# Reciprocals as exp(-ln), dealt feature steps, a weight chunk on another queue and a last product in halves: one change to a gated mix of two attention blocks

## Chip, core and metric

The kernel runs on one core of a Trainium2 chip. The metric is device time in microseconds (us): the median of repeated executions of the whole program. Beside these times there is one profiled execution, whose trace gives the start and length of each instruction on each engine.

The engines are named as the profile names them: PE is TensorE (PEld its weight loads), DVE is VectorE, ACT is ScalarE, POOL is GpSimd, SP is SyncE, which here only issues DMAs. A "q" after a name is the engine's own queue or sequencer.

## What is computed

Two attention blocks read the same x (2048 rows, 1024 columns, 32 heads of 32). A is a linear attention with the feature map phi, B a local one that looks at 8 earlier positions, 2 apart. A sigmoid gate mixes them. (The weights and x are bf16. `z` is the einsum as it stands, a sum over the sequence.)

```python
def A(x, wqkv, wo):
    q, k, v = split_heads(x @ wqkv)
    phi = lambda t: jnp.where(t > 0, t + 1, jnp.exp(t)) + 1e-6
    pq, pk = phi(q), phi(k)
    kv = jnp.einsum("bhsd,bhse->bhde", pk, v)
    z = jnp.einsum("bhsd->bhd", pk)
    num = jnp.einsum("bhqd,bhde->bhqe", pq, kv)
    den = jnp.einsum("bhqd,bhd->bhq", pq, z)[..., None] + 1e-6
    return heads_to_rows(num / den) @ wo

def B(x, wqkv, wo):
    q, k, v = split_heads(x @ wqkv)
    # logits over 8 gathered keys, 2 apart, masked below 0
    attn = softmax(logits * Dh ** -0.5)
    return heads_to_rows(attn @ gathered_v) @ wo

g = sigmoid((x * gate_w).sum(-1, keepdims=True))
out = g * A(x, A_wqkv, A_wo) + (1 - g) * B(x, B_wqkv, B_wo)
```

## The kernel before

**Products.** x is transposed by DMA into xT (`xt_load`, L89 to L92). Even and odd rows of x are kept apart (`xpar`), since B looks back in steps of 2. Most of the large products are done in a seven-product scheme of 2x2 blocks (class `Group`, L236): products m1 to m7 of sums and differences of blocks of x and of the weights, accumulated in PSUM tiles X and Y, with intermediate saves M1s, U2s and U4s by ScalarE (`save`, L256) and evacuations by VectorE that add a save to a PSUM tile (`acc`, L228). The sums of x and of the weights are VectorE operations at L102 to L105 and L133 to L136. `run` (L393) interleaves the products of one group with m3 and m4 of the group before. PSUM holds four banks for these products (X0, X1, Y0, Y1), and one slot of four banks (`side_ps`, L323) that everything else shares: B's scores `s`, B's attention output `o`, A's key-value product `kps`, A's output `oA`.

**Order.** The order on TensorE and on SP is that of the program text. The instructions of the other engines are put in order by a scheduler that respects dependencies. After each product `side` (L350) moves the program's own clock on by one step and does two things. It deals one VectorE operation from lists that were handed to `defer` (L361), placed behind the last evacuation (`dve_side`, L371). And it may advance one of the side generators: B's attention (`attn`, L641), A's key-value product (`kv`, L526), A's output (`out` in `qa_out`, L564).

**Stages by the profile's clock.** Up to 24 us: B's value projection of the first pairs in plain form (`vb_plain`, L464), while DMAs bring x and the first weights, and warm-up matmuls (`warm_up`, L431) fill the wait. To 66 us: the rest of B's values and the first keys and queries. To about 303 us: B's keys and queries by columns, alternating with A's keys and values by rows, and B's attention in between. To about 356 us: A's queries in plain form (`qa_plain`, L605) with A's output. To 387 us: the last queries together with the first output products. To the end: the output products of eight pairs (`out_group`, L783). The last pair's group has `last` set, which puts m5 ahead of m7; its last product is m4.

**First loads.** SP issues, in this order, the transpose of x tile 0, the four chunks of the first half of B's value weights (`vb_load(k, 0)`, 256 KB each), the transposes of tiles 4, 1 and 5, the four chunks of the second half, and further transposes (L184 to L193). ScalarE's first instruction is a table load (L79).

**A's key features.** When one row tile of A's keys is complete, `done` in `ka_group` calls `phi` (L498): an Exp on ScalarE (L500) and three VectorE operations, the maximum with 0 (L504), the minimum with 1 plus eps (L505), and the sum (L506). They are issued at once, all three together. There are 16 such tiles. The `kv` generator of the same pair, one or more groups later, reads the result.

**A's output.** For each 128 columns of queries and each half (16 times), `out` multiplies the query features `eq` with KVz (L575), ScalarE copies the PSUM result to `of` or `ofv` (L577), GpSimd adds eps to the 33rd column of each head (L580) and multiplies by `nel` (L581), VectorE takes the reciprocal (L583), and GpSimd multiplies the numerators by it in two operations (L586). A store to DRAM follows (L588). `nel` holds exp(-gate), so that dividing by it gives the gate's ratio g/(1-g); the factor 1-g (`omg`) is applied at the very end. The query features are made of an Exp by ScalarE (L622) and VectorE operations (L625, L627), which release the PSUM bank.

**The end.** Each output tile is evacuated by `final` of `out_group` (L806 to L814), by ScalarE or VectorE into `osb` (128x512), and stored by SP.

Of the kernel before, what the change touches and what calls it, by code (L numbers as in the profile page):

```python
# [8 lines left out]
ACT = mybir.ActivationFunctionType  # L9
ALU = mybir.AluOpType  # L10
# [3 lines left out]
F32 = mybir.dt.float32  # L14
P = 128
# [3 lines left out]
SPAN = 3 * TW  # L19
EPS = 1e-6  # L20
RATE_R = 0.8
RELU_ACT = (False, False)
OA_DELAY = 5
RATE_Q = 1.0
RATE_O = 1.3
# [3 lines left out]
def kernel(  # L29
# [11 lines left out]
    nc = tc.nc  # L41
# [11 lines left out]
    outpar = out[0].rearrange("(j p) d -> p j d", p=2)  # L53

    def xrows(t):
        return xpar[t // 8, (t % 8) * P:(t % 8 + 1) * P, :]

    consts = ctx.enter_context(tc.tile_pool(name="consts", bufs=1))
# [10 lines left out]
    ps_pj = ctx.enter_context(tc.tile_pool(name="ps_pj", bufs=1, space=bass.MemoryType.PSUM))  # L69
# [19 lines left out]
    def xt_load(t):  # L89
        p, j = divmod(t, 8)  # L90
        hf, c = divmod(j, 4)
        nc.sync.dma_start_transpose(out=xT[p][:, :, hf, c * P:(c + 1) * P], in_=xrows(t))  # L92
# [81 lines left out]
    W = wp.tile([P, 8, D], BF16, name="W", tag="W")  # L174
# [4 lines left out]
    nc.gpsimd.dma_start(out=gw[:], in_=gate_w.rearrange("(k p) -> p k", p=P))  # L179

    def vb_load(k, j):
        nc.sync.dma_start(out=W[:, 2 * k:2 * k + 2, 512 * j:512 * j + 512],
                          in_=bview[:, 2 * k:2 * k + 2, 2 * D + 512 * j:2 * D + 512 * j + 512])
    xt_load(0)  # L184
    for k in range(4):
        vb_load(k, 0)
    for t in (4, 1, 5):
        xt_load(t)
# [30 lines left out]
    nc.gpsimd.memset(bd[:], 0.0)  # L219
    for i in range(4):  # L220
        nc.gpsimd.memset(bd[32 * i:32 * i + 32, i, :], 1.0)
    nel = consts.tile([P, 16], F32, name="nel")
    omg = consts.tile([P, 16], F32, name="omg")
    KVz = consts.tile([P, 8, 132], BF16, name="KVz")

    last_dve = [None]

    def acc(out_, ps, add):  # L228
        if add is None:
            nc.scalar.copy(out=out_, in_=ps)  # L230
        else:
            last_dve[0] = nc.vector.tensor_tensor(out=out_, in0=ps, in1=add, op=ALU.add).ins  # L232
# [3 lines left out]
    class Group:  # L236
# [37 lines left out]
        def m6(self):  # L274
            self.mm(self.X, 6, False)
            self.U2s = self.save(self.X, "U2s", self.scale[1])

        def m7(self):
            self.Y = self.ps("Y")
            self.mm(self.Y, 7, True)  # L280
            if self.last:
                self.final(1, 1, self.Y[:], self.U4s[:])

        def m5(self):
            self.mm(self.X, 5, False)
# [8 lines left out]
                self.row_done(0)  # L294

        def m4(self):
            self.mm(self.Y, 4, False)
            self.final(1, 0, self.Y[:], self.U2s[:])
            if self.row_done:
                self.row_done(1)  # L300

    def row_ops(w, pair):
        p, c = divmod(pair, 4)
        return lambda m, kc: (xop(m, kc, p, slice(c * P, c * P + P)), w.get(m, kc))
# [18 lines left out]
    def side_ps(name):  # L323
        return ps_s.tile([P, 4, 512], F32, name=name, tag="s")
# [36 lines left out]
    def defer(products, ops, gap=1):  # L361


        deferred.append([state["now"] + products, list(ops), gap])
# [46 lines left out]
    def tile_of(pair, i):  # L411
        return (pair // 4) * 8 + (pair % 4) + 4 * i
# [3 lines left out]
    gps = gps_tile[:, 0, 0:16]  # L416
# [6 lines left out]
                             start=kc == 0, stop=kc == 7)  # L423

    def gate_end():
        nc.scalar.activation(out=nel[:], in_=gps, func=ACT.Exp, scale=-1.0)
        nc.scalar.activation(out=omg[:], in_=gps, func=ACT.Exp)
        nc.vector.tensor_scalar(out=omg[:], in0=omg[:], scalar1=1.0, scalar2=None, op0=ALU.add)
        nc.vector.reciprocal(out=omg[:], in_=omg[:])
# [65 lines left out]
                    vb_store(vs[pair], pair, i)  # L495


    def phi(e, t, relu_on_act=False):  # L498

        nc.scalar.activation(out=e, in_=t, func=ACT.Exp)  # L500
        if relu_on_act:
            nc.scalar.activation(out=t, in_=t, func=ACT.Relu)
        else:
            nc.vector.tensor_scalar(out=t, in0=t, scalar1=0.0, scalar2=None, op0=ALU.max)  # L504
        nc.vector.tensor_scalar(out=e, in0=e, scalar1=1.0, scalar2=EPS, op0=ALU.min, op1=ALU.add)  # L505
        nc.vector.tensor_tensor(out=e, in0=e, in1=t, op=ALU.add)  # L506

    pks = {}
    kv_state = {"n": 0}
# [1 line left out]
    def ka_group(w, pair):  # L511
        ts = [tring.tile([P, D], BF16, name="tA", tag="t") for _ in range(2)]

        def final(i, j, ps, add):
            acc(ts[i][:, 512 * j:512 * j + 512], ps, add)

        def done(i):
            e = ering.tile([P, D], BF16, name="eA", tag="e")
            phi(e[:], ts[i][:])
            pks[tile_of(pair, i)] = e  # L520
        return Group(row_ops(w, pair), final, done)

# [34 lines left out]
    def cols_of(ap, nn, n=1):  # L557

        return ap.rearrange("(n r) (c e) -> r n c e", n=n, c=4)[:, :, nn, :]
# [3 lines left out]
    def qa_out(es, nn, p):  # L563
        def out(i):  # L564
            yield 0, 2
            oa["n"] += 1
            if oa["n"] % 3 and not any(e[4] == "attn" for e in queue):
                of = vwp.tile([P, 4, 8, 33], F32, name="ofv", tag="vw")
            else:
                of = ofp.tile([P, 4, 8, 33], F32, name="of", tag="of", bufs=1)  # L570
            rec = smallp.tile([P, 4, 8, 1], F32, name="rec", tag="rec")
            o = side_ps("oA")
            for k in range(4):
                for j in range(2):
                    nc.tensor.matmul(o[:, k, 132 * j:132 * j + 132], lhsT=es[i][:, j, k * P:(k + 1) * P],  # L575
                                     rhs=KVz[:, nn + 4 * j, :], start=True, stop=True)
            oa["copy"] = nc.scalar.copy(out=of[:].rearrange("p n h e -> p n (h e)"), in_=o[:, :, 0:264]).ins  # L577
            yield 1, 2
            t = 8 * p + 4 * i
            nc.gpsimd.tensor_scalar(out=rec[:, :, :, 0], in0=of[:, :, :, 32], scalar1=EPS, scalar2=None, op0=ALU.add)  # L580
            nc.gpsimd.tensor_tensor(out=rec[:, :, :, 0], in0=rec[:, :, :, 0],  # L581
                                    in1=nel[:, t:t + 4, None].broadcast_to([P, 4, 8]), op=ALU.mult)
            nc.vector.reciprocal(out=rec[:], in_=rec[:])  # L583
            ob = tring.tile([P, 4, 8, 32], BF16, name="obA", tag="t")
            for k in range(0, 4, 2):
                nc.gpsimd.tensor_tensor(out=ob[:, k:k + 2], in0=of[:, k:k + 2, :, 0:32],  # L586
                                        in1=rec[:, k:k + 2].broadcast_to([P, 2, 8, 32]), op=ALU.mult)
            nc.sync.dma_start(out=cols_of(OA_d[p][i][:, :], nn, 4),  # L588
                              in_=ob[:].rearrange("p k h e -> p k (h e)"))
        return out  # L590

    def qa_group(w, nn, p):
        ts = [tring.tile([P, 2, 512], BF16, name="tq", tag="t") for _ in range(2)]
        es = [ering.tile([P, 2, 512], BF16, name="eq", tag="e") for _ in range(2)]
        out = qa_out(es, nn, p)

        def final(i, j, ps, add):
            acc(ts[i][:, j, :], ps, add)

        def done(i):  # L600
            phi(es[i][:], ts[i][:], RELU_ACT[i])
            add_side(OA_DELAY, out(i), p, "oa")
        return Group(col_ops(w, p), final, done)

# [178 lines left out]
    def out_group(pair, parts):  # L783
        p, c = divmod(pair, 4)

        def operands(m, kc):
            assert m in (1, 2, 4) or ("o", id(parts)) in ready, (pair, m)
            n, c4 = divmod(kc, 4)
            o, S, o16, n0 = parts[min(n, len(parts) - 1)]
            n -= n0  # L790
            if m == 1:
                l = o[:, 0, n, 2 * c4]
            elif m == 2:
                l = o[:, 0, n, 2 * c4 + 1]
            elif m == 4:
                l = o[:, 1, n, 2 * c4 + 1]
            elif m == 7:
                l = o16[:, 1, n, 2 * c4]
            else:
                l = S[:, {5: 0, 6: 1, 3: 2}[m], n, c4]  # L800
            return l, Wo["AB"[n + n0]].get(m, c4)

        ts = [tile_of(pair, i) for i in range(2)]
        sc = [omg[:, t:t + 1] for t in ts]

        def final(i, j, ps, add):  # L806
            osb = ering.tile([P, 512], BF16, name="osb", tag="e")
            if add is None:
                nc.scalar.activation(out=osb[:], in_=ps, func=ACT.Copy, scale=sc[i])
            else:  # L810
                last_dve[0] = nc.vector.scalar_tensor_tensor(out=osb[:], in0=ps, scalar=sc[i], in1=add,  # L811
                                                             op0=ALU.mult, op1=ALU.add).ins
            r0 = (ts[i] % 8) * P
            nc.sync.dma_start(out=outpar[p, r0:r0 + P, 512 * j:512 * j + 512], in_=osb[:])  # L814
        return Group(operands, final, nk=8, scale=sc)


# [67 lines left out]
    cols = []  # L885
# [75 lines left out]
```

## Time and profile before

| | |
|---|---|
| median of 8 runs | 468.33 us (467.1 to 469.31) |
| profiled execution | 467.51 us |
| its span, first to last instruction | 465.6 us |
| granted TensorE clock | 1.0 throughout |
| 66 to 303 us: TensorE / VectorE / ScalarE busy | 229.7 / 160.4 / 154.2 us of 237 |
| 303 to 356 us: TensorE / VectorE / ScalarE / GpSimd | 50.1 / 39.7 / 25.8 / 34.9 us of 53 |
| 387 to 462 us: TensorE / VectorE / ScalarE | 74.7 / 25.7 / 17.2 us of 75 |

The 1.9 us between the profiled execution's time and its span lie outside the first and last instruction. Busy times of different engines overlap; an engine that is idle costs nothing unless another waits for it. Matmul ends are modelled in the profile: a 128x512 matmul is shown with 379 ns while eight in a row take 1.73 us, that is 0.216 us each.

How the lines below are read: a timeline line has start, duration (both us), engine, source line, operation, output tile, input tiles, shapes, and in brackets the idle time ahead of it with the instruction that ended it. A line of the waits table has who waited, for whom, and then us in total, number of times, and the longest.

### The profile page before, as it was taken

The page shows a single profiled execution, that of the slowest core. Times are in us where ns is not written, and L with a number is a line of the kernel's source. Part 1 is how long each engine was busy: PE and PEld are TensorE (multiplying, and loading weights), DVE is VectorE, ACT ScalarE, POOL GpSimd, SP SyncE. Part 2 cuts the span into 40 slices and gives each one's busy share as a digit, 9 for nine tenths or more (in the row PEclk, how much of TensorE's full clock was granted, in tenths as well). Part 3 has the DMA queues.
Part 4 walks back from the last instruction along what each step waited for, and adds up shares of the span by engine and source line. Part 5 has one row for each costly group of instructions (what it writes and reads, how often), then busy time and mean ns, then how long its engine had stood idle before and what let it go on. Part 6 is the DMA issues. An engine that isn't in the chain of part 4 may idle for free. (4 is left out here: it accounts for less than half of the span.)

```text
span 465.6 us, 11844 instructions
## 1 busy us (share of the span) xinstructions
PE 447.0 (96%) x5052; PEld 217.3 (47%) x5129; DVE 280.6 (60%) x458; ACT 230.2 (49%) x331; POOL 65.1 (14%) x145
## 2 busy tenths in 40 slices
PE   7989999999999999999999999999989999999997
PEld 5445444444444444444444444445545444444443
DVE  0546668769748587485774847578767763155211
ACT  1233447568468385683855848535554432222221
POOL 8000000000000000000000000008887521000000
PEclk9999999999999999999999999999999999999999
DMA  7999811590301703017020075373229971598111
GB/s 169 194 216 240 276 43 64 149 251 18 80 4 34 157 19 74 11 32 156 19 72 14 24 157 185 84 209 80 68 75 201 210 160 58 105 194 199 45 46 45
DMA packets 117653, 51.65 MB, mean 111 GB/s; under 512 B 77664, under 2 KB 115552, under 8 KB 117600
## 3 DMA queue, kind: packets, MB, share of 16 engines
q1 hardware_dynamic: 117504, 50.88, 46.8%
q8 instruction: 40, 0.66, 0.6%
q0 software_dynamic: 96, 0.01, 0.1%
q14 instruction: 13, 0.11, 0.1%
HBM read 25.69 MB, written 16.79 MB: 91 GB/s over the span
## 5 line engine op out<-in xcount | busy, mean ns | idle before, releaser
L617 PE MATMUL Q<-xT,WS 128*128 128x512 bf16 x246 | 57.7, 379 | 2.9 <-DVE eq L627 1.7
L250 PEld LDWEIGHTS <-xT 128*128 128x128 bf16 (+1 forms) x352 | 32.6, 98 | 38.3 <-issue 1.5
L250 PE MATMUL X<-T,SS 128*128 128x512 f16 x176 | 45.2, 379 | 0.0
L660 ACT ACTIVATE PT<-s 128x1368 bf16<-128x1368 f32 x24 | 31.5, 1311 | 20.1 <-PE s L654 20.0
L259 ACT COPY U4s<-X 128x512 f32<-128x512 f32 x38 | 22.1, 581 | 35.5 <-PE X L250 35.5
L250 PE MATMUL Y<-W,xT 128*128 128x512 bf16 (+1 forms) x143 | 37.4, 379 | 1.9 <-issue 1.1
L617 PEld LDWEIGHTS <-WS 128*128 128x128 bf16 x256 | 24.3, 98 | 29.4 <-issue 3.0
L250 PEld LDWEIGHTS <-WS 128*128 128x128 bf16 (+1 forms) x256 | 24.0, 98 | 29.2 <-issue 2.0
L250 PEld LDWEIGHTS <-SS 128*128 128x128 f16 x264 | 24.4, 98 | 27.8
L622 ACT ACTIVATE eq<-Q 128x512 bf16<-128x512 f32 x32 | 19.1, 598 | 32.0 <-PE Q L617 30.9
L662 DVE TENSOR_TENSOR PT<-PT,maskp 128x1368 bf16<-128x1368 bf16 x24 | 20.8, 868 | 20.8 <-ACT PT L660 20.8
L250 PE MATMUL Y<-xT,WS 128*128 128x512 bf16 (+1 forms) x128 | 32.9, 380 | 0.0
L250 PE MATMUL X<-SS,TS 128*128 128x512 f16 x128 | 32.8, 379 | 0.0
L250 PEld LDWEIGHTS <-oT 128*128 128x128 bf16 (+1 forms) x192 | 18.8, 98 | 22.8 <-issue 0.3
L250 PEld LDWEIGHTS <-TS 128*128 128x128 f16 x192 | 18.2, 98 | 22.1 <-issue 1.1
L259 ACT COPY M1s<-X 128x512 f32<-128x512 f32 x38 | 22.2, 584 | 11.8 <-PE X L250 9.1
L259 ACT COPY U2s<-X 128x512 f32<-128x512 f32 x38 | 22.1, 582 | 9.1 <-PE X L250 9.1
L685 DVE COPY nB<-o 128x684 f32<-128x684 f32 x24 | 20.8, 867 | 8.0 <-ACT rB L684 7.3
L586 POOL TENSOR_TENSOR obA<-ofv,rec 128x512 bf16<-128x512 f32 x22 | 23.7, 1099 | 8.2 <-DVE rec L583 7.6
L250 PE MATMUL Y<-W,oT 128*128 128x512 bf16 (+1 forms) x96 | 22.7, 379 | 0.0
L250 PE MATMUL X<-T,oS 128*128 128x512 f16 x96 | 22.7, 379 | 0.0
L250 PE MATMUL X<-W,SS 128*128 128x512 bf16 x79 | 22.2, 380 | 0.5
(125 smaller groups left out, 732.8 us busy)
## 6 DMA issues: line engine op xcount, KB each, us to landing
OB_d<-oB SPq DMA_DIRECT2D x24, 171.0 KB, 3.0
V_d<-va SPq DMA_DIRECT2D x16, 256.0 KB, 2.5
WS<-in_B_wqkv_dram SPq DMA_DIRECT2D x16, 256.0 KB, 4.3
W<-in_A_wqkv_dram SPq DMA_DIRECT2D x8, 512.0 KB, 6.1
OA_d<-obA SPq DMA_DIRECT2D x16, 256.0 KB, 2.3
out_dram<-osb SPq DMA_DIRECT2D x32, 128.0 KB, 1.8
oT<-OB_d SPq DMA_DIRECT2D x12, 256.0 KB, 4.8
vw<-V_d SPq DMA_DIRECT2D x8, 288.0 KB, 4.9
```

Of the source, the lines that this page charges most:

```text
L250: nc.tensor.matmul(ps[:], lhsT=lhsT, rhs=rhs, start=start and kc == 0, stop=kc == self.nk - 1, skip_group_check=True)
L259: nc.scalar.copy(out=s[:], in_=ps[:])
L586: nc.gpsimd.tensor_tensor(out=ob[:, k:k + 2], in0=of[:, k:k + 2, :, 0:32], in1=rec[:, k:k + 2].broadcast_to([P, 2, 8, 32]), op=ALU.mult)
L617: nc.tensor.matmul(ps[:], lhsT=w.W[:, kc, j * P:j * P + P], rhs=xT[p][:, kc, i, :], start=kc == 0, stop=kc == 7, skip_group_check=True)
L622: nc.scalar.activation(out=es[i][:, j, :], in_=ps[:], func=ACT.Exp)
L660: nc.scalar.activation(out=PT[:], in_=s[:, :, 0:TW], func=ACT.Exp, scale=SCALE)
L662: nc.vector.tensor_tensor(out=PT[:], in0=PT[:], in1=m[:, None, :].broadcast_to([P, 4, TW]), op=ALU.mult)
L685: nc.vector.tensor_copy(out=nB[:], in_=o[:, 0:4:2, 0:TW])
```

## The change

Five edits (names and lines are those of the kernel before, where it has them):

1. A's output. GpSimd's addition of eps and VectorE's reciprocal are gone. ScalarE now takes Ln of the denominator, with eps as its bias operand (a new 128x1 constant that GpSimd fills at the start), and then Exp of minus that, which is the reciprocal. GpSimd multiplies by `nel`, and `nel` is now exp(+gate), so that multiplying takes the place of dividing. The two multiplications by the numerators stay.
2. A's key features. `phi` issues its Exp and returns the three VectorE operations as a list. For A's keys the list goes to `defer(0, ...)`, so one is dealt per product, each behind the last evacuation. For the query features of `qa_group`, a function that the program does not use in its present plan, they are issued at once as before. The constant RELU_ACT, which was false for both, is gone.
3. The first chunk of the first weights is issued from ScalarE's queue, ahead of everything on SP; SP goes on with the transpose of x tile 0 and the other three chunks.
4. In the last group, m7 and m4 are each done in two halves of 256 columns. The halves lie in two PSUM banks (Y of this group and Y of the one before), and each half has its own evacuation and its own store.
5. `final` takes a range of columns for that.

```diff
     def vb_load(k, j):
-        nc.sync.dma_start(out=W[:, 2 * k:2 * k + 2, 512 * j:512 * j + 512],
+        (nc.scalar if (k, j) == (0, 0) else nc.sync).dma_start(out=W[:, 2 * k:2 * k + 2, 512 * j:512 * j + 512],
                           in_=bview[:, 2 * k:2 * k + 2, 2 * D + 512 * j:2 * D + 512 * j + 512])
+    vb_load(0, 0)
     xt_load(0)
-    for k in range(4):
+    for k in range(1, 4):
         vb_load(k, 0)
...
+    eps = consts.tile([P, 1], F32, name="eps")
+    nc.gpsimd.memset(eps[:], EPS)
...
+        def half(self, m, k, add, j):
+
+            h = slice(256 * k, 256 * k + 256)
+            if m == 7:
+                self.Ys.append(ps_pj.tile([P, 512], F32, name="Y", tag="Y" + str((self.par + k) % 2)))
+            for kc in range(self.nk):
+                lhsT, rhs = self.operands(m, kc)
+                nc.tensor.matmul(self.Ys[k][:, h], lhsT=lhsT, rhs=rhs[:, h], start=m == 7 and kc == 0,
+                                 stop=kc == self.nk - 1, skip_group_check=True)
+            self.final(1, j, self.Ys[k][:, h], add[:, h], h)
+
         def m7(self):
+            if self.last:
+                self.Ys = []
+                for k in range(2):
+                    self.half(7, k, self.U4s, 1)
+                return
             self.Y = self.ps("Y")
             self.mm(self.Y, 7, True)
-            if self.last:
-                self.final(1, 1, self.Y[:], self.U4s[:])
...
         def m4(self):
+            if self.last:
+                for k in range(2):
+                    self.half(4, k, self.U2s, 0)
+                return
...
     def gate_end():
-        nc.scalar.activation(out=nel[:], in_=gps, func=ACT.Exp, scale=-1.0)
+        nc.scalar.activation(out=nel[:], in_=gps, func=ACT.Exp)
...
-    def phi(e, t, relu_on_act=False):
+    def phi(e, t):
 
         nc.scalar.activation(out=e, in_=t, func=ACT.Exp)
-        if relu_on_act:
-            nc.scalar.activation(out=t, in_=t, func=ACT.Relu)
-        else:
-            nc.vector.tensor_scalar(out=t, in0=t, scalar1=0.0, scalar2=None, op0=ALU.max)
-        nc.vector.tensor_scalar(out=e, in0=e, scalar1=1.0, scalar2=EPS, op0=ALU.min, op1=ALU.add)
-        nc.vector.tensor_tensor(out=e, in0=e, in1=t, op=ALU.add)
+        return [lambda: nc.vector.tensor_scalar(out=t, in0=t, scalar1=0.0, scalar2=None, op0=ALU.max),
+                lambda: nc.vector.tensor_scalar(out=e, in0=e, scalar1=1.0, scalar2=EPS, op0=ALU.min, op1=ALU.add),
+                lambda: nc.vector.tensor_tensor(out=e, in0=e, in1=t, op=ALU.add)]
...
             e = ering.tile([P, D], BF16, name="eA", tag="e")
-            phi(e[:], ts[i][:])
+            defer(0, phi(e[:], ts[i][:]))
...
-            nc.gpsimd.tensor_scalar(out=rec[:, :, :, 0], in0=of[:, :, :, 32], scalar1=EPS, scalar2=None, op0=ALU.add)
+            nc.scalar.activation(out=rec[:, :, :, 0], in_=of[:, :, :, 32], func=ACT.Ln, bias=eps[:, 0:1])
+            nc.scalar.activation(out=rec[:, :, :, 0], in_=rec[:, :, :, 0], func=ACT.Exp, scale=-1.0)
             nc.gpsimd.tensor_tensor(out=rec[:, :, :, 0], in0=rec[:, :, :, 0],
                                     in1=nel[:, t:t + 4, None].broadcast_to([P, 4, 8]), op=ALU.mult)
-            nc.vector.reciprocal(out=rec[:], in_=rec[:])
...
-        def final(i, j, ps, add):
+        def final(i, j, ps, add, cols=slice(0, 512)):
...
-                last_dve[0] = nc.vector.scalar_tensor_tensor(out=osb[:], in0=ps, scalar=sc[i], in1=add,
+                last_dve[0] = nc.vector.scalar_tensor_tensor(out=osb[:, cols], in0=ps, scalar=sc[i], in1=add,
                                                              op0=ALU.mult, op1=ALU.add).ins
             r0 = (ts[i] % 8) * P
-            nc.sync.dma_start(out=outpar[p, r0:r0 + P, 512 * j:512 * j + 512], in_=osb[:])
+            nc.sync.dma_start(out=outpar[p, r0:r0 + P, 512 * j + cols.start:512 * j + cols.stop], in_=osb[:, cols])
```

More of the change, by code (lines that the diff above doesn't have):

```diff
@@ L21 @@
 RATE_R = 0.8
-RELU_ACT = (False, False)
 OA_DELAY = 5
@@ L600, in done @@
         def done(i):
-            phi(es[i][:], ts[i][:], RELU_ACT[i])
+            for f in phi(es[i][:], ts[i][:]):
+                f()
             add_side(OA_DELAY, out(i), p, "oa")
```

## The prediction, made before the changed kernel ran

> **What bounds the kernel now.** I read the busy shares first, then TensorE's waits, then the timeline around each wait.
>
> ```profile
> span 465.6 us, 11844 instructions
> ## 1 busy us (share of the span) xinstructions
> PE 447.0 (96%) x5052; PEld 217.3 (47%) x5129; DVE 280.6 (60%) x458; ACT 230.2 (49%) x331; POOL 65.1 (14%) x145
> ```
>
> TensorE is busy 96% of the span at full clock; nothing in the change removes a matmul. So the change can win only what lies in TensorE's 18.6 us of gaps (465.6 - 447.0) and at the two ends. The table of waits for TensorE alone (us in total, times, longest) says who ends those gaps:
>
> ```profile
> PE s L654 <- DVE nB L685: 2.0, 6, 0.7
> PE Q L617 <- DVE eq L627: 1.7, 1, 1.7
> PE gps L422 <- DMA xT<-in_A_x_dram: 1.6, 2, 1.0
> PE K L475 <- DMA W<-in_B_wqkv_dram: 1.3, 1, 1.3
> ...
> PE Y L250 <- DVE vA L232: 0.6, 1, 0.6
> PE Q L617 <- DVE vA L232: 0.5, 1, 0.5
> ```
>
> Four parts of the change face four of these places. Middle (100 to 300 us), one of the six score waits:
>
> ```profile
> 140.59 0.72 ACT L684 ACTIVATE rB<-o 128x684 f32<-128x684 f32 x1
> 140.91 0.42 DVE L504 TENSOR_SCALAR tA<-tA 128x1024 bf16<-128x1024 bf16 x1
> ...
> 141.58 0.86 DVE L685 COPY nB<-o 128x684 f32<-128x684 f32 x1
> ...
> 142.49 0.56 PE L654 MATMUL s<-qT,kT 32*64 32x57 bf16 x48 [0.27 <-DVE nB L685]
> ```
>
> Columns are start, length, engine and line, tiles. The numerator copy nB empties the one PSUM slot that scores, PV, KV and A's output share. It stands on VectorE behind A's feature steps (L504, then L505) although the Ln it also waits for ended at 141.31; TensorE stands 0.27 us. A's query stage:
>
> ```profile
> 346.77 0.24 POOL L581 TENSOR_TENSOR rec<-rec,nel 128x32 f32<-128x32 f32 x1
> ...
> 347.04 0.35 DVE L583 RECIPROCAL rec<-rec 128x32 f32<-128x32 f32 x1 [2.89 <-POOL rec L581]
> 347.31 0.36 DVE L625 TENSOR_SCALAR eq<-eq 128x1024 bf16<-128x1024 bf16 x1
> ...
> 348.45 2.75 PE L617 MATMUL Q<-xT,WS 128*128 128x512 bf16 x12 [1.68 <-DVE eq L627]
> ```
>
> VectorE runs in order: the reciprocal waits 2.89 us for GpSimd, the feature steps of the next query tile stand behind it, and TensorE waits 1.68 us for their PSUM banks. GpSimd is late because one output takes it L580 1.17 + L581 0.24 + two L586 of 1.05 + VectorE's 0.35 and hand-overs = 4.15 us (starts of L580 at 333.96 and 338.11), while TensorE brings one every 3.9 us (oA at 331.73, 335.64). The head and the tail:
>
> ```profile
> 7.57 0.59 PE L475 MATMUL K<-W,xT 128*128 128x512 bf16 x2 [1.26 <-DMA W<-in_B_wqkv_dram]
> ```
>
> ```profile
> 462.26 0.75 DVE L811 SCALAR_TENSOR_TENSOR osb<-Y,omg,U2s 128x512 bf16<-128x512 f32 x1 [2.65 <-PE Y L250]
> ```
>
> The first product waits 1.26 us for the first weight chunk. After the last matmul only a 0.75 us evacuation, a 0.33 us issue and a store of about 1.7 us to landing remain.
>
> [...] Ln (L684) and Exp (L686) alternate 24 times, and the only table load is at 0.72 us. [...] L580 takes 0.32 us alone and 1.17 beside VectorE's weight sums, which take 1.75 there and 1.22 elsewhere. [...] here an issue of this chunk takes 0.45 to 0.58 us.
>
> **The change part by part.**
>
> *A's reciprocals.* Removed per output: L580 (0.32 to 1.17 us on GpSimd) and L583 (0.35 us on VectorE, with its wait); added: a Ln and an Exp of 128x32 on ScalarE. [...] the nearest row, the 128x16 Exp of L426, is 0.185. With hand-overs 0.6 us an output, 16 outputs. Behind them on ScalarE stand the next query Exp (L622) or M1s. Cover: after the copy ScalarE idles 0.66 us until the next Q is there (313.90 to 314.55), and 1.13 us before the Exp after that. So 0.6 us just fits; if it doubled, the first Exp would slip by about 0.6 and the next would absorb it, since TensorE needs the pair only a tile later. GpSimd falls to 0.24 + 2.1 = 2.4 us an output, under 3.9, so its backlog is gone, and VectorE no longer waits for it at all. What is late next at 346.77? Query features there need the Exp of 343.05, done at 343.65, so they can end by 345.3; the bank is free before TensorE asks. The 1.68 us goes; the 0.34 us wait for the copy at 341.38 stays. Bounds: 0 (another wait takes over) to 2.0; I take 1.7. The earlier output stores are worth nothing more: from 348.45 to 462 TensorE shows gaps of 0.05 us only. The sign change of nel costs nothing, the eps memset falls in GpSimd's start-up.
>
> *Feature steps dealt out.* Same three VectorE operations (0.42, 0.42, 0.69 us), 16 times, now one per product step after an evacuation. The order of instructions in the changed kernel shows nB one or two steps earlier in every A-key group; ScalarE's order there is unchanged, so nB can start no earlier than the end of its Ln. Wait by wait, with nB starting 0.02 after the Ln and taking 0.86: at 112.38 Ln ends 111.33, scores could start at 112.25, gain 0.13 of 0.66; at 142.49, 201.04 and 259.58 the whole 0.27 each; at 230.25 0.15; at 289.04 Ln ends 287.74, the whole 0.40. The 0.61 at 117.89 is vA's evacuation standing behind a mask product (116.36, 0.86 us) that it now precedes, and fewer operations before: all of it. Sum 0.13 + 0.81 + 0.15 + 0.40 + 0.61 = 2.1. Against it: the delayed steps return ahead of the second nB. Walked through by hand with the trace's durations around 170 to 180, the second nB still starts at 176.4, where its Ln ends, because VectorE uses the time it had idled; around 118 it starts at 117.8 against 118.08. The features themselves finish up to 8 us later, but the KV product that reads the first ones ran at 126.5 against features ready at 99.5, so that is covered. Bounds: 2.1 won to 1.0 lost; I take 1.8, allowing for a small new wait or two. The 0.49 us at 304.54 has no feature steps before it and stays.
>
> *First weight chunk on ScalarE.* One issue moves off SP; behind it on SP all chunks and transposes come 0.53 us earlier. ScalarE has nothing to do until 10.48, so nothing is queued behind it there. Unknown: whether the issue starts at 0.72 beside the table load, or after it at 2.0[...]. Chunks landed about 5.4 to 5.9 us after their issues at 2.13, 2.70 and so on, that is at 7.5, 8.3, 8.9, 9.6; TensorE used them at 7.57, 8.33, 9.09, 9.85, and tile 4 landed at 10.57 for 10.59. Early issue: the later chunks and tile 4 each 0.5 earlier, gain about 0.5, though the first wait is 1.26. Late issue: first chunk as before, gain about 0. Bounds: 1.26 won, 0.5 lost (the chunk competes with the transposes). I take 0.3. The waits on xT near 30 us move along, as those loads follow stores of the first products.
>
> *Last product in halves.* 32 matmuls of 256 columns replace 16 of 512. Three 128x256 warm-ups fill 8.00 to 8.33, 0.11 us each, half of 0.216 for 512, so TensorE pays nothing. The last evacuation covers 256 columns[...]. The first half's goes under the second half's matmuls (0.86 us). The final store is half the bytes, perhaps 0.05 less. The second bank belongs to the previous group and was emptied a product before. Bounds 0.1 to 0.6; I take 0.3.
>
> Sum: 1.7 + 1.8 + 0.3 + 0.3 = 4.1 us. The profiled execution took 467.51, so 463.4 in its terms; the median shown is 468.33, 0.8 above it (the eight runs lie near 467.3 and near 469.1), and the forecast for the median is 468.33 - 4.1 = **464.2 us**.
>
> **Rivals.** (1) *The score waits stay*: nB's Ln, or something else on ScalarE, ends the wait, and the dealt steps only move it. For: the Ln ends just 0.02 to 0.4 us before nB starts now. Against: five of six waits close by the calculation. Then 4.1 - 1.8 = 2.3 won, 466.0. (2) *Query stage bound by ScalarE*: Ln and Exp are longer than 0.6 and the PSUM wait at 346.77 comes back through L622 or the copy. For: only 0.06 us of cover in the first gap. Against: 1.13 us in the next. Then 2.4 won, 465.9. (3) *Slower*: the dealt steps stand ahead of evacuations TensorE needs, one mechanism at the shared slot and the Y banks of the A-key groups. At 0.4 us for each of 16 features it costs 6.4, with 2.3 from the other parts: 4.1 lost, 472.4; it decides from 2.3/16 = 0.14 us a feature on. For: VectorE is busy 42.6 of the 54 us from 66 to 120. Against: the walk-through. (4) *ScalarE's issue is early and the chunks land in full*: 1.0 more won, 463.2; this lies inside the forecast's own range.
>
> **How the numbers follow.** Forecast with (4) 0.70, rival (1) 0.11, (2) 0.09, slower (3) 0.06, and 0.04 for no visible change because several parts fail together. A measurement tells 0.3%, 1.4 us, from no change. Forecast, (1) and (2) mostly lie below 466.9: faster 0.85, same 0.08, slower 0.07. The range goes from all upper bounds together (2.0 + 2.1 + 1.26 + 0.6 = 6.0 won, 462.4), with 0.6 us for the spread that the eight runs show, to rivals (1) and (2) with 1 us for it, 467.0.
>
> **What would show it.** Right: no reciprocal on VectorE after 312 us, no TensorE wait on eq, GpSimd idle between outputs; "s <- nB" down from 2.0 to about 0.5 us; the first product before 7.5 us; a last evacuation near 0.48 us. Wrong: new waits of TensorE on VectorE in 100 to 300 us, ScalarE's L622 starting late against Q, or a table load between Ln and Exp.

## The result, and the profile after

The changed kernel takes 464.58 us (median of 11 runs, 463.23 to 466.24) where the kernel before takes 467.83 us (32 runs): a ratio of 0.9925, with a 95% interval from 0.991 to 0.994. The forecast was 464.2 us.

Each kernel's times lie in two groups: in some executions the granted TensorE clock falls to half, for 3.4 us in each of the five profiles that show it (a dip; the mean clock of the run is then 0.995 or 0.996), and such a run is 1.3 to 2.3 us longer, so groups of the same kind are compared:

| | runs without a dip | runs with a dip |
|---|---|---|
| before (93 runs beside the experiments) | 467.54 (58) | 469.18 (35) |
| after | 463.50 (6) | 465.78 (6) |

So the change is worth 4.0 us without a dip and 3.4 us with one. The profiled execution of after (464.94 us, span 463.1; it is counted in the table) has a dip, that of before has none. A mean clock of 0.998 or 0.999 is not counted as a dip: in the profile of experiment 5, with 0.998, the clock is 1.00 up to 460 us and 0.66 from there to 465, and the last product has ended at 458.22.

The head of the page of after: TensorE is busy 1.7 us more although it does the same arithmetic, which is as much as the dip costs. GpSimd has lost 9 us, ScalarE has gained 8.

```profile
span 463.1 us, 11880 instructions
## 1 busy us (share of the span) xinstructions
PE 448.7 (97%) x5068; PEld 219.5 (47%) x5145; DVE 280.1 (60%) x444; ACT 238.2 (51%) x363; POOL 56.3 (12%) x130
```

TensorE's waits in after (us in total, times, longest):

```profile
PE gps L442 <- DMA xT<-in_A_x_dram: 1.6, 2, 1.2
...
PE s L672 <- DVE nB L703: 0.6, 1, 0.6
...
PE oA L592 <- ACT ofv L594: 0.3, 1, 0.3
...
PE K L495 <- DMA xT<-in_A_x_dram: 0.3, 1, 0.3
PE Y L252 <- DVE qT L234: 0.2, 1, 0.2
```

The wait on eq (1.7) is gone, the one on W (1.3) is gone, and so is that of Y on vA (0.6). nB is down from 2.0 to 0.6. Two small waits are new (K on xT, Y on qT), and the 1.6 us on the input tiles are as large as before.

A score stage in after, in the timeline, which answers to the one at 142.49 in before:

```profile
141.26 0.72 ACT L702 ACTIVATE rB<-o 128x684 f32<-128x684 f32 x1
141.57 0.42 DVE L521 TENSOR_SCALAR tA<-tA 128x1024 bf16<-128x1024 bf16 x1
...
142.01 0.87 DVE L703 COPY nB<-o 128x684 f32<-128x684 f32 x1
142.08 0.81 PE L252 MATMUL X<-W,xT 128*128 128x512 bf16 x3
142.69 0.57 ACT L261 COPY U4s<-X 128x512 f32<-128x512 f32 x1
142.94 0.56 PE L672 MATMUL s<-qT,kT 32*64 32x57 bf16 x48
```

nB now starts within 0.03 us of its Ln's end (141.98), one feature step earlier in VectorE's order, and the scores show no idle time.

The query stage in after, where before stood 1.68 us:

```profile
346.86 0.35 ACT L597 ACTIVATE rec<-ofv,eps 128x32 f32<-128x32 f32 x1
347.00 0.43 DVE L643 TENSOR_SCALAR eq<-eq 128x1024 bf16<-128x1024 bf16 x1 [1.36 <-ACT eq L640]
347.24 0.23 ACT L598 ACTIVATE rec<-rec 128x32 f32<-128x32 f32 x1
...
347.54 0.24 POOL L599 TENSOR_TENSOR rec<-rec,nel 128x32 f32<-128x32 f32 x1 [1.00 <-ACT rec L598]
...
348.63 0.62 PE L592 MATMUL oA<-KVz,eq 128*128 128x132 bf16 x8
349.09 1.67 PE L635 MATMUL Q<-xT,WS 128*128 128x512 bf16 x6
```

GpSimd now waits for ScalarE (1.00 us here, 0.8 to 1.6 us at twelve of the thirteen outputs from 318 to 364 us) instead of VectorE waiting for GpSimd, and TensorE goes on without a stop. The head and the tail:

```profile
0.77 0.42 ACTq L181 DMA_DIRECT2D W<-in_B_wqkv_dram  x1
...
6.30 0.73 PE L495 MATMUL K<-W,xT 128*128 128x512 bf16 x2
```

```profile
457.77 1.91 PE L287 MATMUL Y<-T,oT 128*128 128x256 f16 x16
...
459.72 0.48 DVE L829 SCALAR_TENSOR_TENSOR osb<-Y,omg,U2s 128x256 bf16<-128x256 f32 x1 [0.39 <-PE Y L287]
```

The chunk's issue starts at 0.77, beside ScalarE's table load (0.74, 1.28 us long), and the chunk lands at 3.7. The first product starts at 6.30 instead of 7.57, right behind the warm-up products and no longer behind the chunk. The last evacuation takes 0.48 us. But from the start of the last product to the end of the span there are 5.33 us here (463.1 - 457.77) and 5.27 in before (465.6 - 460.33):

```profile
460.33 1.89 PE L250 MATMUL Y<-T,oT 128*128 128x512 f16 x8
```

What took some of it back in this execution is seen in the table by stretches of 1 us (PEclk is the third number from the end):

```profile
29.00:30.00 1.00, 0.12 (x5) 0.12 (x6) 0.92 (x3) 0.00 (x0) 0.00 (x0) 1.00 1.03 168
30.00:31.00 1.00, 1.00 (x11) 0.44 (x10) 0.00 (x0) 0.00 (x0) 0.00 (x0) 0.73 1.29 188
31.00:32.00 1.00, 0.78 (x3) 0.45 (x3) 0.00 (x0) 0.33 (x1) 0.00 (x0) 0.50 1.05 200
32.00:33.00 1.00, 1.00 (x4) 0.31 (x3) 0.00 (x0) 0.26 (x1) 0.00 (x0) 0.50 0.95 118
33.00:34.00 1.00, 1.00 (x4) 0.36 (x3) 0.57 (x1) 0.00 (x0) 0.00 (x0) 0.56 1.24 254
```

The missing clock adds up to 0.27 + 0.50 + 0.50 + 0.44 = 1.71 us of work. It begins after TensorE has waited 0.42 and 1.20 us for the input tiles of 28.33 and 29.88.

### The profile page after: what moved, and what is told of

Read it like the earlier page. It is cut to its first block, busy times and chain, and to the rows that moved or that the text cites. A ratio compares the mean times of both kernels' runs of the same rounds, so it can differ in the third digit from the quotient of the medians.

```text
span 463.1 us, 11880 instructions
## 1 busy us (share of the span) xinstructions
PE 448.7 (97%) x5068; PEld 219.5 (47%) x5145; DVE 280.1 (60%) x444; ACT 238.2 (51%) x363; POOL 56.3 (12%) x130
## 5 line engine op out<-in xcount | busy, mean ns | idle before, releaser
L252 PEld LDWEIGHTS <-oT 128*128 128x128 bf16 (+1 forms) x176 | 17.2, 98 | 20.8
L643 DVE TENSOR_SCALAR eq<-eq 128x1024 bf16<-128x1024 bf16 x16 | 12.3, 768 | 17.2 <-ACT eq L640 17.2
```

Source lines behind the costliest of these rows:

```text
L252: nc.tensor.matmul(ps[:], lhsT=lhsT, rhs=rhs, start=start and kc == 0, stop=kc == self.nk - 1, skip_group_check=True)
L643: nc.vector.tensor_scalar(out=e[:], in0=e[:], scalar1=1.0, scalar2=EPS, op0=ALU.min, op1=ALU.add)
```

## The experiments

First each part of the change alone, put on the kernel before; then the waits at 28 to 31 us; then a version that is faster than both kernels, and its parts.

**1. The reciprocals alone.** Only the edit in A's output (with eps and the sign of nel).

> The kernel before with the reciprocals of A's output as exp(-ln) on ScalarE alone. Forecast's theory (TensorE's wait for the scores' evacuation at 348 us goes and nothing takes its place): 1.7 us less than before, no TensorE wait on VectorE's eq, oA outputs 3.9 us apart, clock-independent. Rival (ScalarE becomes the bound of the query stage): 0 to 0.4 us less, with TensorE waits on ScalarE's Exp or ofv there. In this kernel alone nothing else of the head or of the feature steps moves, so the waits for nB (2.0 us), for W (1.3 us) and for vA (0.6 us) should stay as they were.

Measured: 465.65 us without a dip (11 runs) against 467.54, so 1.9 us less; the ratio is 0.9962 [0.9948, 0.9975]. The wait on eq is gone, oA outputs follow at 3.92 us (346.58, 350.50, 354.41), and no wait of TensorE on ScalarE has grown. Its profiled run has a dip, so the lead is read at the same instructions, in before and then in this kernel:

```profile
345.29 0.62 PE L575 MATMUL oA<-KVz,eq 128*128 128x132 bf16 x8
351.04 0.62 PE L575 MATMUL oA<-KVz,eq 128*128 128x132 bf16 x8
```

```profile
346.58 0.62 PE L577 MATMUL oA<-KVz,eq 128*128 128x132 bf16 x8
350.50 0.62 PE L577 MATMUL oA<-KVz,eq 128*128 128x132 bf16 x8
```

At the first oA this kernel is 1.29 us behind before, at the next 0.54 ahead: 1.83 us won. That is 0.15 more than the 1.68 listed, because a listed wait starts at the modelled end of the last matmul (1.03 us for four), later than its real pace of 4 x 0.216.

**2. The dealt feature steps alone.** Only `phi`'s list and `defer(0, ...)`.

> The kernel before with only the key feature steps dealt out behind evacuations. Forecast's theory: waits of the scores' products for nB fall from 2.0 us to about 0.6 us and the one for vA of 0.6 us goes, together 1.8 to 2.1 us less. Rival (waits stay, ended by ScalarE's Ln): 0 to 0.3 us less. Rival (dealt steps hold up the evacuations behind them): slower by up to 4 us. The waits for W (1.3 us) and eq (1.7 us) stay.

Measured: 466.14 without a dip (7 runs), 1.4 us less; ratio 0.9981 [0.9969, 0.9993]. The listed waits fell as foreseen, nB to 0.6 and vA to nothing, which is 2.0 us. Only 1.4 us arrived. The distance to before at each score stage (this kernel is 1.33 us late from its head on, where it has a dip) shows where:

| instruction | before | dealt alone | behind by | won since the line above |
|---|---|---|---|---|
| scores | 112.38 | 113.61 | 1.23 | 0.10 |
| kps after vA | 126.51 | 127.62 | 1.11 | 0.12 |
| scores | 142.49 | 143.38 | 0.89 | 0.22 |
| scores | 171.70 | 172.50 | 0.80 | 0.09 |
| scores | 201.04 | 201.62 | 0.58 | 0.22 |
| scores | 230.25 | 230.73 | 0.48 | 0.10 |
| scores | 259.58 | 259.84 | 0.26 | 0.22 |
| scores | 289.04 | 288.96 | -0.08 | 0.34 |

Every nB gain that was forecast is there to within 0.06 of its own estimate, and 0.09 came at 171.70, where none was. The vA gain is 0.12 in place of 0.61. The second nB in before, and this kernel's timeline after that place, show what came instead:

```profile
118.08 0.86 DVE L685 COPY nB<-o 128x684 f32<-128x684 f32 x1
```

```profile
118.69 0.69 DVE L502 TENSOR_TENSOR eA<-eA,tA 128x1024 bf16<-128x1024 bf16 x1
...
119.30 0.86 DVE L682 COPY nB<-o 128x684 f32<-128x684 f32 x1
...
120.68 0.86 DVE L685 TENSOR_TENSOR oB<-nB,rB 128x684 bf16<-128x684 f32 x1
...
123.09 0.57 ACT L258 COPY M1s<-X 128x512 f32<-128x512 f32 x1
...
123.70 1.02 PE L249 MATMUL X<-SS,TS 128*128 128x512 f16 x4
...
125.07 0.68 DVE L231 TENSOR_TENSOR qT<-Y,M1s 128x512 bf16<-128x512 f32 x1
...
125.81 1.02 PE L249 MATMUL Y<-xT,WS 128*128 128x512 f16 x4 [0.22 <-DVE qT L231]
```

The second nB starts at 119.30, behind a feature step. Set back by the 1.23 us that this run is late, that is 118.07: no earlier than in before (118.08), while TensorE had come 0.61 us closer to it. The chain behind it (oB, ScalarE's next Ln and Exp, its copy M1s, then qT) stops TensorE twice: 0.23 us at 123.70, which no wait lists (the four before it started at 122.61 and fill 0.86), and 0.22 us at 125.81.

**3. The first weight chunk alone.**

```diff
-        nc.sync.dma_start(out=W[:, 2 * k:2 * k + 2, 512 * j:512 * j + 512],
+        (nc.scalar if (k, j) == (0, 0) else nc.sync).dma_start(out=W[:, 2 * k:2 * k + 2, 512 * j:512 * j + 512],
...
+    vb_load(0, 0)
     xt_load(0)
-    for k in range(4):
+    for k in range(1, 4):
```

> The kernel before with only the first weight chunk issued by ScalarE. Theory A (the lead reaches the end): the first product about 1.2 us earlier, the fourth tile's about 0.9 us earlier, and about 0.9 us less in the end. Theory B (the lead is given back at the input tiles of about 28 to 31 us, which come when the queue brings them): the two waits for input tiles there grow by what was won, and the end moves by 0 to 0.3 us. Theory C (longer idle waits there also draw the clock down): a granted clock of 0.5 to 0.7 in the slices at 30 to 34 us in the profile of a run with a mean clock of 0.996 instead of 1.0, and such a run 1.5 to 2 us longer than one without.

Measured: 467.17 without a dip (6 runs, 466.62 to 468.40), 0.4 us less, and a ratio of 1.0003 [0.9986, 1.002], which can't be told from no change. The timeline shows why the head's 1.3 to 2 us never arrive:

```profile
5.58 0.59 PE L476 MATMUL K<-W,xT 128*128 128x512 bf16 x2
6.01 0.49 PE L434 MATMUL gps<-KVacc 128*128 128x256 bf16 x3
7.77 0.59 PE L476 MATMUL K<-W,xT 128*128 128x512 bf16 x2 [1.27 <-DMA W<-in_B_wqkv_dram]
```

The first product starts 2.0 us earlier than in before, and the second waits 1.27 us for the second chunk. At that second product 0.56 us are left (before: 8.33), at the scores of 67 us 0.3. This profile has no dip, although TensorE waited 0.87 and 0.91 us for the input tiles. So waiting there doesn't always bring one; the last section has these waits profile by profile.

**4. The last product in halves alone.**

> The kernel before with only the last product in halves. Forecast's theory: last evacuation 0.48 us instead of 0.75, end 0.3 us earlier. Rival (the store's own time sets the end and the smaller evacuation is lost in the two halves' own starts): 0 to 0.1 us. Both lie near the size of the run-to-run spread, so the trace from the last product's start to the end of the span decides: 0.3 us shorter, or the same.

Measured: 467.50 without a dip, against 467.54; ratio 1.0001 [0.9986, 1.0015]. Nothing, then. The end of its timeline:

```profile
462.01 1.91 PE L285 MATMUL Y<-T,oT 128*128 128x256 f16 x16
...
463.95 0.48 DVE L829 SCALAR_TENSOR_TENSOR osb<-Y,omg,U2s 128x256 bf16<-128x256 f32 x1 [0.39 <-PE Y L285]
```

The evacuation is 0.27 us shorter, but from its end to the end of the span it takes 2.97 us (467.4 - 464.43), against 2.59 in before (465.6 - 463.01). The sync queue's waits after 455 us name the place: its last wait, for the store, is 1.3 us here and in after, and 1.0 in before and in experiments 1 to 3, although the half store lands in 1.6 us after its issue and the whole one in 1.7. Why the smaller store is waited for longer stays open.

**5 and 6. Fillers ahead of the late input tiles.** Throwaway products keep TensorE busy while it waits; the result is not touched.

```diff
     x_loads(6, 7)
-    gates(4)
+    warm_up(4)
+    gate(tile_of(4, 0))
+    warm_up(10)
+    gate(tile_of(4, 1))
```

> The changed kernel, with 4 and 10 throwaway groups of warm-up products put on TensorE ahead of the two products that wait for the input tiles of about 28 to 30 us, so that TensorE hardly idles there although the tiles come as late as before. The result computed is unchanged. Theory (the idle waits at 28 to 30 us provoke the clock's dip at 30 to 35 us, worth 1.6 us): no dip there, every run at a mean clock of 1.0 (or with a dip elsewhere only rarely), runs in one cluster near 463.5. Rival (the dip comes at some moment of the first 35 us whatever stands idle): two clusters as before, some 40 to 50 of 100 runs at a clock of 0.996 and 1.6 to 2.3 us longer. If the fillers themselves hold up the real products, both clusters lie up to 1 us later.

> The kernel before with the same fillers ahead of the same two waits. Theory (idle waits provoke the dip): one cluster near 467.5, no run near 469.1. Rival (the dip comes anyway): still about 4 of 10 runs near 469.1 at a clock of 0.996.

Measured on the changed kernel: 463.44, five runs from 463.33 to 463.87, none with a dip. On the kernel before: 467.61 without a dip, and 2 of 14 runs with one (469.16), where 35 of 93 have one without fillers. These counts are small, but with those at the end of this section they make waiting at 28 to 31 us one cause of the dip. It is not the only one: in the kernel before, the wait for the first chunk was left in place. That a dip can come there too is seen in experiment 2, in its timeline

```profile
7.50 1.01 PE L474 MATMUL K<-W,xT 128*128 128x512 bf16 x2 [2.25 <-DMA W<-in_B_wqkv_dram]
```

and in its table by stretches of 1 us:

```profile
7.00:8.00 1.00, 0.50 (x2) 0.22 (x2) 0.00 (x0) 0.00 (x0) 0.93 (x6) 0.62 1.10 359
8.00:9.00 1.00, 1.00 (x6) 0.54 (x5) 0.00 (x0) 0.00 (x0) 0.80 (x4) 0.50 1.65 173
9.00:10.00 1.00, 1.00 (x4) 0.40 (x3) 0.00 (x0) 0.00 (x0) 0.73 (x4) 0.50 0.86 184
10.00:11.00 1.00, 1.00 (x7) 0.57 (x5) 0.00 (x0) 0.00 (x0) 0.94 (x6) 0.68 1.11 250
```

Again 0.38 + 0.50 + 0.50 + 0.32 = 1.70 us of clock are missing.

**7. An input pair's load moved ahead on the sync queue.** In the profile of after, the v_b stores wait 2.8 us on that queue for ScalarE's va, and the transposes of the next input tiles stand behind them.

```diff
+    x_loads(4)
     vb_plain(0, 1)
-    x_loads(4, 5)
+    x_loads(5)
```

> The changed kernel with the loads of one input pair issued ahead of one pair of v_b stores' loads on the sync queue, so that the tiles that TensorE waits for at 28 to 30 us come about 2 us earlier. Theory (the lead won at the head is given back at these waits): the 1.6 us of waiting for them goes to under 0.4 us, and undipped runs come down from 463.5 to about 462. With the theory that idle waits provoke the dip, dipped runs get rare as well. Rival (the queue only shifts the wait to the next loads): the same 463.5, with a wait of the same size for the later tiles or for the v_b loads.

Measured: 461.54 us (461.24 to 461.62, four runs, none with a dip), ratio 0.9861 [0.9842, 0.988] to the kernel before. The wait on xT is gone from TensorE's table, and the sync queue's wait for va in 15 to 32 us is 0.8 us. It is 2.0 us less than after without a dip: the 1.6 us listed, and most of the rest may be what listed waits leave out (an estimate: 1.03 - 4 x 0.216, about 0.17 us for each of the two).

**8. A second Ln and Exp for each output.**

```diff
             nc.scalar.activation(out=rec[:, :, :, 0], in_=rec[:, :, :, 0], func=ACT.Exp, scale=-1.0)
+            rec2 = smallp.tile([P, 4, 8, 1], F32, name="rec2", tag="rec2")
+            nc.scalar.activation(out=rec2[:, :, :, 0], in_=of[:, :, :, 32], func=ACT.Ln, bias=eps[:, 0:1])
+            nc.scalar.activation(out=rec2[:, :, :, 0], in_=rec2[:, :, :, 0], func=ACT.Exp, scale=-1.0)
```

> The changed kernel with a second Ln and a second Exp of each of A's outputs on ScalarE, written to a tile that nobody reads: 0.58 us more of ScalarE for each of the 16 outputs, 9.3 us in all. Forecast's theory (ScalarE has slack in the query stage beside TensorE's 3.9 us for an output): at most 0.3 us longer. Rival (ScalarE's order decides when evacuations start, and so the bound of that stage): 0.2 to 0.6 us for an output, 3 to 9 us longer.

Measured: 463.91 without a dip, 0.4 us more than after, a little over the forecast's bound and far from the rival's. In 312 to 390 us TensorE waits for the same single thing as in after, the 0.3 us on ofv, and from its first oA to its last 66.25 us pass in both (311.61 to 377.86 in after, 310.61 to 376.86 here). The extra 0.4 us, of three runs, lies outside that stage; in the profiles the input tiles come 0.7 us later here (29.02 and 30.55) than in after, which may be it. One pair of operations costs less than the sum of their lengths, since the second Ln begins 0.24 us after the first (346.10 and 345.86), which is 0.35 us long. So ScalarE has room for twice the added work.

**9. Experiment 7 without the early chunk.**

> The changed kernel with the earlier input load (461.5 us), but with the first weight chunk back on the sync queue. Theory (the head is worth about 0.4 us wherever no later wait takes it back, since the second product then waits for the second chunk): 0.3 to 0.6 us longer, 461.8 to 462.1. Rival (the first product's 1.3 to 2 us lead counts in full): 1.2 us or more longer. Rival (the lead is swallowed at some later load): no change.

Measured: 462.32 without a dip (4 runs of 6), 0.8 us longer than experiment 7, more than foreseen. In the profiles, tile 4's products start at 10.54 here and at 10.05 there: 0.5 us of it is the head. Another 0.4 is a wait of Y on an osb evacuation that the profile of 7 doesn't have. Such waits on osb (0.3 to 0.6 us) come and go between runs.

**10. The moved load on the kernel before.**

> The kernel before with only the earlier input load. Theory (the 1.6 us of waiting for the tiles of 29 to 31 us is all there is to win, and it goes whole): 465.6 to 466.0, and no run with the clock's dip at 30 to 35 us. Rival (the wait only moves to another load): 467.2 to 467.5, with dipped runs near 469.1.

Measured: 465.87 without a dip, 1.7 us less. Three of ten runs still have a dip (467.13). The profiled one has it from 7.3 to 10.7 us, about the end of a 2.17 us wait for the first chunk (7.47), and none at 30 us, as expected. But taking away the wait at 30 us doesn't take away the dips.

**11. Experiment 7 with the last product whole.**

> The changed kernel with the earlier input load, but with the last product whole again. Reading of the trace (the smaller last evacuation's 0.27 us is lost again between it and the end of the span): the same as 461.5 within 0.2. Forecast's theory (halves win 0.3 us): 0.3 us longer, 461.8.

Measured: 461.74 (five runs, 461.62 to 462.93), 0.2 us above experiment 7. In the profiles there are 5.35 us from the last product's start to the end of the span in both (459.7 - 454.35 and 459.8 - 454.45). The halves win nothing that can be seen.

**12. Experiment 7 with the feature steps two products later.**

```diff
-            defer(0, phi(e[:], ts[i][:]))
+            defer(2, phi(e[:], ts[i][:]))
```

> The changed kernel with the earlier input load, and with the key feature steps due two products later than dealt at present, which at the pair after 110 us puts the second numerators' copy (nB) one step further ahead on VectorE. Theory (the 0.61 us won at vA was given back because a feature step stood ahead of that nB, and TensorE then waits 0.22 us for qT and about as long for an X buffer that ScalarE's copy frees): up to 0.4 us less, 461.1 to 461.4, the wait on qT near 125 us gone. Rival (the feature steps come too late for the key sums at other pairs, or hold up other evacuations): 0.2 to 1 us longer.

Measured: 461.53 (461.12 to 461.66), the same as experiment 7. The two timelines show that the cause was right and that the gain was lost elsewhere. kps starts at 123.14 against 123.86: 0.72 us earlier, of which 0.10 was there before the scores, so 0.62 is won at this place, and the wait on qT is gone. First experiment 7, then this one:

```profile
123.86 0.68 PE L554 MATMUL kps<-vA,eA 128*32 128x33 bf16 x64
```

```profile
123.14 0.68 PE L554 MATMUL kps<-vA,eA 128*32 128x33 bf16 x64
```

The lead stays 0.71 us to the scores at 255. Then the last pair gives back 0.4, in a stall amid the products with PT:

```profile
287.66 0.28 PE L690 MATMUL o<-PT,vw 64*32 64x57 bf16 x25
...
288.36 0.28 PE L690 MATMUL o<-PT,vw 64*32 64x57 bf16 x23 [0.41 <-issue]
```

"issue" means that the profile shows nobody who was waited for. What holds these products is open. The 0.3 us that are left show in the two profiled spans (459.5 and 459.8), but not in the medians.

All runs with a clock on record, by the two waits; each field has the runs with a dip, and in brackets the kernels:

| | input tiles late | tiles earlier, or covered by fillers |
|---|---|---|
| first chunk from the sync queue | 68 of 151 (before, 1, 2, 4) | 7 of 30 (6, 9, 10) |
| first chunk from ScalarE | 15 of 30 (after, 3, 8) | 0 of 19 (5, 7, 11, 12) |

Treating the tiles takes most dips away. The early chunk alone doesn't; with it, and the tiles treated, none is left.

## Why the prediction was right, and where it was not

The time (464.2 forecast, 464.58 measured) and the sum without a dip (4.1 forecast, 4.0 measured) agree. Some of that closeness is luck. The forecast started from a median of 8 runs that 32 runs put 0.5 us lower, the median of after is the slowest of its runs without a dip, and by the two medians the change is worth 3.25 us. The terms' errors cancel in part too:

| term | forecast | alone on before, no dip |
|---|---|---|
| reciprocals | 1.7 | 1.9 |
| dealt steps | 1.8 | 1.4 |
| first chunk | 0.3 | 0.4 (single runs spread over 1.8) |
| halves | 0.3 | 0.0 |
| sum | 4.1 | 3.7 (together, in after: 4.0) |

The 0.3 us between 3.7 and 4.0 are not assigned to anything by these runs.

The **reciprocals** went as worked out. Ln took 0.352 us and Exp 0.229, and at 346.86 in after the two together 0.61, where the author had estimated 0.6 with hand-overs; no wait took the place of the 1.68, and the 0.3 us on the copy stayed. Experiment 8 answers the rival of a query stage bound by ScalarE: double the load leaves that stage's waits as they were. The forecast put the next features' end by 345.3 and said that VectorE would no longer wait for GpSimd, and no such wait is in the trace. What it lacked is the 0.15 us that a listed wait understates.

The **dealt steps** were right for nB, wait by wait, also in the 0.6 that stays at 113.17 (forecast 0.53). The step that failed is "all of it" for the 0.61 at 117.89. The walk-through asked whether the second nB would start later, and it did not (117.8 forecast, 118.07 measured). It should have asked whether TensorE, once 0.61 us ahead, would now meet that unmoved chain, and it does. Experiment 12 confirms the reading: with the steps later, the missing 0.5 us appears at that place.

The **first chunk** landed early (3.7 us), which was the side held open: its issue ran beside the table load. The limit named, that the later chunks come only 0.5 us earlier, is what experiment 3 shows (0.56 left at the second product). The waits on xT move along in after, where they are as long as before and lie 0.8 to 1 us earlier. In experiment 3 they do so only in part: they lie 0.15 and 0.25 us earlier and are 0.22 longer in sum.

The **halves** were mis-sized. The evacuation took 0.48 us, as the author had estimated, and the 16 matmuls of the last product took 1.91 us where the eight took 1.89, but the store's "perhaps 0.05 less", an estimate too, is measured as 0.3 to 0.4 more between the evacuation and the end of the span (2.97 and 2.59 us).

The rival that was slower, dealt steps ahead of evacuations, has its mechanism in the trace, but at one place of eight and for 0.45 us. The dip was not foreseen. The forecast noted that the eight runs lie near 467.3 and near 469.1 without asking why.

## What to carry to other kernels

When a stall goes, follow the engine that is now early to the next thing it needs, and ask whether that has moved as well; if not, only the difference is won. Check a lead at the same instruction in two traces, not by the sum of listed waits: here they missed a stall of 0.23 us (123.70 in experiment 2) and understated another by 0.15 (experiment 1). In a kernel bound by TensorE, look at the granted clock by microseconds before explaining two groups of times, and at what stands in a DMA queue ahead of a load that TensorE waits for.

## What the runs showed of the hardware

- In the five profiles with a dip (after, experiments 1, 2, 4 and 10), the clock missed 1.70 to 1.71 us each time, that is 3.4 us at half. The clock falls once more after the last product: in after at 463.95, 4.3 us behind that product's end at 459.68.

```profile
463.00:464.00 1.00, 0.00 (x0) 0.00 (x0) 0.00 (x0) 0.00 (x0) 0.00 (x0) 0.98 0.00 0
464.00:465.00 1.00, 0.00 (x0) 0.00 (x0) 0.00 (x0) 0.00 (x0) 0.00 (x0) 0.50 0.02 8
```

- Similar waiting brings a dip in one run and not in another. These are TensorE's two waits for the input tiles, in the profiles that have them:

| profile | first, second wait (us) | sum | dip behind them |
|---|---|---|---|
| after | 0.42, 1.20 | 1.62 | yes |
| experiment 1 | 0.73, 0.87 | 1.60 | yes |
| experiment 4 | 0.83, 0.71 | 1.54 | yes |
| before | 0.54, 1.02 | 1.56 | no |
| experiment 2 | 0.79, 0.76 | 1.55 | no (its dip is at the head) |
| experiment 3 | 0.87, 0.91 | 1.78 | no |
| experiment 8 | 0.41, 1.17 | 1.58 | no |

- At the head, the waits for the first chunk of 2.25 us (experiment 2) and 2.17 (experiment 10) have a dip that begins in their last 0.3 us (at 7.24 and 7.34); those of 1.26 (before), 1.55 (experiment 9) and 1.92 (experiment 4) have none. What decides, here and at the tiles, was not shown.
- The profile of before has a clock of 1.0 throughout, but in the first microseconds that doesn't fit TensorE's pace. In before, 24 warm-up products of 256 columns take from 1.18 to 6.31 us, 0.21 us each, where three take 0.33 us later (8.00 to 8.33). In experiment 2 they end at 5.25, in 4 at 5.62. The earlier they end, the longer TensorE stands before the first chunk: 1.26 us in before, 2.25 in experiment 2 and 1.92 in 4. Why their pace differs was not shown.
- ScalarE issued a DMA at 0.77 us, while its table load (0.74 to 2.02) and the sync queue's first transpose (0.75 to 2.11) were under way. It took 0.42 us, and the chunk landed 2.9 us after it.
- A feature step on VectorE (128x1024) took 1.23 us instead of 0.43 beside GpSimd's multiplications (343.09 and 347.00 in after); from 303 to 390 us the mean is 0.79, and it was 0.38 in before. Seven of these steps in after took 1.10 to 1.25 us, each with a multiplication under way beside it, and none in before took more than 0.43. Why they take longer there was not shown. TensorE has no wait on eq in after.
